# Linear-attention and SwiGLU kernel: zeros on TensorE ahead of the first tile, a written order for four token tiles, phi's small add on GpSimd

## Chip, cores and metric

One Trainium2 chip, one of its cores. The metric is the time of one execution in microseconds (us), as the device reports it; lower is better. Of the profiled execution, the span runs from the first to the last instruction of the program.

## What is computed

A block of x (2048 tokens by 1024, bf16) is layer-normalised, put through linear attention with 32 heads of 32 columns, and gated by a SwiGLU network whose output goes through one more silu:

```python
xn = layernorm(x)                      # eps 1e-5
q, k, v = split(xn @ wqkv)             # 32 heads of 32
phi = lambda t: where(t > 0, t + 1, exp(t)) + 1e-6
kv = einsum("bhsd,bhse->bhde", phi(k), v)
z = einsum("bhsd->bhd", phi(k))
o = einsum("bhqd,bhde->bhqe", phi(q), kv) / (phi(q) . z + 1e-6)
s = o @ wo
g = silu((silu(xn @ w_gate) * (xn @ w_up)) @ w_down)    # F = 3584
out = x + s * g
```

The sums kv and z run over all 2048 tokens, so no query can be finished before the last token's K and V are known.

## The kernel before

**Stages.** Tokens go in 16 tiles of 128 (four to a block). Stage 1, the K/V stage: each tile is normalised to `xn` (fp16), transposed on TensorE (`emit_A2`, L289; eight 128x128 transposes into one PSUM bank, copied to `xnT` by VectorE, L300), then multiplied with four chunks of 512 columns of the K/V weights `wkv_sb` (`emit_B`, L315; eight matmuls a chunk, L322): chunks 0 and 1 are K, 2 and 3 are V. A K chunk goes through phi (`emit_phi`, L121): ScalarE takes exp (L123) and relu (L125) of the PSUM bank into `e_t` and `r_t`, VectorE adds 1e-6 to `r_t` (L126) and forms min(e_t, 1) + r_t (L127). A V chunk is copied by ScalarE (L330). `emit_C` (L333) multiplies phi(k) with V into `kvz_ps`, eight small products a tile. From token 1024 on, `xn` is transposed by a DMA over `xn_dram` (L310, L311) instead of TensorE. Stage 2: 32 products for q (`emit_Q`, L142, phi again), products with kv and z (`emit_ND`, L416) and, after a DMA transpose of o, the product with wo (`emit_S`, L449), whose result goes to `s_dram`. The first eight Q tiles run before the first `emit_ND`; VectorE forms the first sums of FFN weights (`sum_w`, L629 to L633) beside them. Stage 3 is the FFN as seven products of halves (L511), two thirds of the time.

**Normalisation.** `emit_stats` (L233) makes two `bn_stats` and one `bn_aggr` a tile. Tiles 0 and 1 take the root on ScalarE (`emit_rstd_act`, L255). Tiles 2 and 3 one by one, and later tiles four together, take it by three Newton rounds on VectorE (`emit_rstd`, L262), operations on 128x1 or 128x4. `emit_norm` (L283) applies it.

**Buffers.** PSUM: `psB` has three banks for K/V chunks, q and s products; `psC` two for transposes; `psA` three for kvz. `e_t`, `r_t`, `xn` and `pk_sb` have two buffers each, V two (`v_bufs`).

**What sets the order.** Each engine runs its own list in order. In stages 1 and 2 a planner with its own costs writes the lists from the program's order and the dependencies; the loop at L362 gives that order: tile i's chunk 0, `emit_C` of tile i - 1, the other chunks, then tile i + 2's normalisation and transposes. In VectorE's list that comes out as the first half of tile 2's `bn_stats` ahead of tile 1's `bn_aggr`. In stage 3 the order of TensorE and GpSimd is written out by hand.

**Loads.** SyncE (SP) issues x tile 0 (its second half is issued by ScalarE, L188), K/V chunk 0 in two halves, then x1, chunk 1, x2, chunk 2, x3, chunk 3, x4 and the other x tiles (L200 to L209). `wq_sb` and `wo_sb` (L210, L212) and the stores to `s_dram` (L462) are issued from GpSimd's queue (POOL). Gates hold x8 on until tile 1's first chunk, wq until tile 3's, wo until tile 5's.

Of the kernel before, what the change touches and what calls it, by code (L numbers as in the profile page):

```python
# [9 lines left out]
ACT = mybir.ActivationFunctionType  # L10
ALU = mybir.AluOpType
# [10 lines left out]
def kernel(  # L22
# [64 lines left out]

    nc.scalar.preload_act_table(ACT.Sqrt)
    ident = persist.tile([P, P], FP16, name="ident")
    make_identity(nc, ident[:])  # L90
# [29 lines left out]

    def emit_phi(work, t_ps, dst, W):  # L121
        e_t = work.tile([P, W], FP32, name="e_t", tag="e_t")
        ex = nc.scalar.activation(out=e_t[:], in_=t_ps, func=ACT.Exp)  # L123
        r_t = work.tile([P, W], FP32, name="r_t", tag="r_t")
        nc.scalar.activation(out=r_t[:], in_=t_ps, func=ACT.Relu)  # L125
        nc.vector.tensor_scalar(out=r_t[:], in0=r_t[:], scalar1=EPS, scalar2=None, op0=ALU.add)  # L126
        nc.vector.scalar_tensor_tensor(out=dst, in0=e_t[:], scalar=1.0, in1=r_t[:],  # L127
                                       op0=ALU.min, op1=ALU.add)
        return ex
# [35 lines left out]
    with ExitStack() as p1:  # L165
# [4 lines left out]
        wkv_sb = wpool.tile([P, DC, 2 * D], BF16, name="wkv_sb")  # L170
        v_bufs = [wpool.tile([P, G, NDW], BF16, name=f"v_sb{k}") for k in range(2)]
        for k in range(2):
            nc.gpsimd.memset(v_bufs[k][:, :, P:P + 1], 1.0)
# [27 lines left out]
        load_wkv(0, halves=2 if DC % 2 == 0 else 1)  # L201
        nx = 1
        for c in range(1, NCH):
# [4 lines left out]
        for i in range(nx, NT):  # L208
            load_x(i)  # L209
        wq_loads = [nc.gpsimd.dma_start(out=wq_sb[:, :, c * CW:(c + 1) * CW], in_=wqkv_v[:, :, c * CW:(c + 1) * CW])  # L210
                    for c in range(NCC)]
        wo_loads = [nc.gpsimd.dma_start(out=wo_sb[:, :, c * CW:(c + 1) * CW], in_=wo_v[:, :, c * CW:(c + 1) * CW])  # L212
                    for c in range(NCC)]
# [19 lines left out]
        def emit_stats(i):  # L233
# [9 lines left out]
            sts = [nc.vector.bn_stats(out=stats[:, c, :], in_=xr[:, c, :]) for c in range(NSC)]  # L243
            if TPB <= i < 2 * TPB:
                late_gates.append((sts, ("B", min(1, NT - 1))))
            nc.vector.bn_aggr(out=mv[:, k, :], in_=stats[:])
# [15 lines left out]
        def emit_rstd(gid):  # L262
            mv, rstd, tiles = grp_state[gid]
            n = len(tiles)
            a = small.tile([P, TPB], FP32, name="lna", tag="lna")
            nc.vector.tensor_scalar(out=a[:, 0:n], in0=mv[:, 0:n, 1], scalar1=EPS_LN, scalar2=None, op0=ALU.add)
            yi = rstd[:, 0:n].bitcast(I32)
            nc.vector.tensor_single_scalar(out=yi, in_=a[:, 0:n].bitcast(I32), scalar=1, op=ALU.arith_shift_right)
            nc.vector.tensor_scalar(out=yi, in0=yi, scalar1=-1, scalar2=0x5f3759df, op0=ALU.mult, op1=ALU.add)
            y = rstd[:, 0:n]  # L270
            w = small.tile([P, TPB], FP32, name="lnw", tag="lnw")
            for _ in range(NR_ITERS):
                if n == 1:
                    nc.vector.scalar_tensor_tensor(out=w[:, 0:1], in0=y, scalar=a[:, 0:1], in1=y,
                                                   op0=ALU.mult, op1=ALU.mult)
                else:
                    nc.vector.tensor_tensor(out=w[:, 0:n], in0=y, in1=y, op=ALU.mult)
                    nc.vector.tensor_tensor(out=w[:, 0:n], in0=w[:, 0:n], in1=a[:, 0:n], op=ALU.mult)
                nc.vector.tensor_scalar(out=w[:, 0:n], in0=w[:, 0:n], scalar1=-0.5, scalar2=1.5,
                                        op0=ALU.mult, op1=ALU.add)  # L280
                nc.vector.tensor_tensor(out=y, in0=y, in1=w[:, 0:n], op=ALU.mult)

# [5 lines left out]

        def emit_A2(i):  # L289
            xn = work.tile([P, D], FP16, name="xn", tag="xn")  # L290
            tr_ps = psC.tile([P, DC, P], FP16, name="tr_ps", tag="C")
            nh = 2 if (i == 0 and DC % 2 == 0) else 1
            dch = DC // nh
            cp = None
            for hh in range(nh):
                cols = slice(hh * dch * P, (hh + 1) * dch * P)
                emit_norm(i, xn[:, cols], cols=(cols if nh > 1 else None))
                for dc in range(hh * dch, (hh + 1) * dch):
                    nc.tensor.transpose(tr_ps[:, dc, :], xn[:, dc * P:(dc + 1) * P], ident[:])  # L299
                cp = nc.vector.tensor_copy(out=xn_tok_ap(i)[:, hh * dch:(hh + 1) * dch, :],  # L300
                                           in_=tr_ps[:, hh * dch:(hh + 1) * dch, :])
            ln_state.pop(i)
            return cp

        def emit_A2_block(b):
# [8 lines left out]

        def emit_B(i, c):  # L315
            if i not in pkv_tiles:
                pk_sb = work.tile([P, D], BF16, name="pk_sb", tag="pk_sb")
                pkv_tiles[i] = (pk_sb, v_bufs[i % 2])
            pk_sb, v_sb = pkv_tiles[i]
            kv_ps = psB.tile([P, CW], FP32, name="kv_ps", tag="B")  # L320
            for dc in range(DC):
                mm = nc.tensor.matmul(kv_ps[:], lhsT=xn_tok_ap(i)[:, dc, :], rhs=wkv_sb[:, dc, c * CW:(c + 1) * CW],  # L322
                                      start=(dc == 0), stop=(dc == DC - 1))
                if dc == 0 and c == 0:
                    marks[("B", i)] = mm
            if c < NCC:
                return emit_phi(phiw, kv_ps[:], pk_sb[:, c * CW:(c + 1) * CW], CW)
            else:
                vc = c - NCC
                return nc.scalar.copy(out=v_sb[:, vc * GPC:(vc + 1) * GPC, 0:P],  # L330
                                      in_=kv_ps[:].rearrange("p (g c) -> p g c", c=P))

# [17 lines left out]
        NPE = min(PE_T_BLOCKS * TPB, NT)  # L350
        cp0 = None
        sq_last = None
        for i in range(min(2, NT)):
            sts = emit_stats(i)
            nstat = i + 1
            if i > 0:
                gate(sts, cp0)
            sq_last = emit_rstd_act(grp_of(i))
            cp = emit_A2(i)
            if i == 0:  # L360
                cp0 = cp
        for i in range(NT):  # L362
            ex = emit_B(i, 0)
            if i == 0:
                gate([ex], sq_last)
            if i > 0:
# [6 lines left out]
            if nxt < NPE:  # L373
                if nxt < TPB:
                    stats_upto(nxt + 1)
                    emit_rstd(grp_of(nxt))
                elif nxt % TPB == 0:
                    stats_upto(nxt + TPB)
                    emit_rstd(grp_of(nxt))
                emit_A2(nxt)  # L380
# [26 lines left out]
    with ExitStack() as p2:  # L407
# [41 lines left out]
        def emit_S(b, t, cc):  # L449
# [10 lines left out]
            if cc == NCC - 1:  # L460
                r0 = b * TB + t * P
                nc.gpsimd.dma_start(out=s_dram[r0:r0 + P, :], in_=s_tiles.pop((b, t))[:])  # L462

# [386 lines left out]
```

## Time and profile before

| what | value |
|---|---|
| time, median of 3 (lowest to highest) | 770.65 us (770.33 to 770.73) |
| profiled execution: time, span | 770.58 us, 768.7 us |
| TensorE (PE) busy | 750.0 us (98%) |
| VectorE (DVE) busy | 485.4 us (63%) |
| ScalarE (ACT) busy | 266.9 us (35%) |
| GpSimd (POOL) busy | 51.8 us (7%) |
| mean granted TensorE clock | 0.996 |

The 1.9 us between time and span lie outside the program's instructions. In the rows of the timeline come: start from the span's start (us), length (us), engine, line, operation, what is written <- what is read, the count of instructions merged into the row, and in brackets the engine's idle time before it with what ended it. A PE row's busy time is modelled, so the spacing of starts tells the pace. PEld is TensorE's weight load; SPq, POOLq are queues that issue DMAs.

### The profile page before, as it was taken

How to read it: one execution, taken by the hardware profiler on the slowest of the kernel's cores; microseconds unless marked ns; L12 is line 12 of the kernel's file. 1: busy time of each engine (PE TensorE's matmuls, PEld its weight loads, DVE VectorE, ACT ScalarE, POOL GpSimd, SP SyncE). 2: the span in 40 equal slices, each digit the busy share in tenths (PEclk: the TensorE clock that was granted, in tenths of full speed). 3: DMA queues.
4: the chain of work that ended last, by engine and by line, in shares of the span. 5: the costliest groups of instructions: out<-in, count | busy, mean ns of one | idle time of the engine just before them, and what ended most of it. 6: DMA issues, size and time to landing. Idle time of an engine off the chain costs nothing.

```text
span 768.7 us, 9747 instructions
## 1 busy us (share of the span) xinstructions
PE 750.0 (98%) x3661; PEld 349.8 (46%) x3696; DVE 485.4 (63%) x987; ACT 266.9 (35%) x461; POOL 51.8 (7%) x61
## 2 busy tenths in 40 slices
PE   5999999999999999999999999999999999999996
PEld 2444444455544444444444444444444444444442
DVE  6994223899760387677876778767655654445542
ACT  2444444555333433433334333343434011111111
POOL 0010000000011000000000000000000221222222
PEclk9999999999999999999999999999999999999999
DMA  9349044014661155553555535453969955544200
GB/s 317 121 155 267 18 108 111 1 41 136 170 203 71 51 160 158 157 170 94 168 150 156 166 104 172 143 153 100 321 185 317 361 179 179 178 177 171 90 28 28
DMA packets 122560, 115.99 MB, mean 151 GB/s; under 512 B 28560, under 2 KB 103184, under 8 KB 121232
## 3 DMA queue, kind: packets, MB, share of 16 engines
q1 hardware_dynamic: 120000, 106.84, 44.8%
q0 software_dynamic: 2368, 8.39, 3.2%
q8 instruction: 29, 0.48, 0.3%
q14 instruction: 19, 0.16, 0.1%
q10 hardware_dynamic: 144, 0.13, 0.0%
HBM read 70.52 MB, written 38.54 MB: 142 GB/s over the span
## 4 chain that ended last, share of the span: by engine, by line
PE 94%; DVE 3%; DMA 1%; issue 1%; SPq 0%; ACT 0%; POOLq 0%; POOL 0%; DVEq 0%
PE X L511 28%; PE Y L511 28%; PE kv_ps L322 12%; PE Z L511 9%; PE q_ps L148 7%; PE s_ps L457 7%; DVE stats L243 2%; DMA xp<-in_A_x_dram 1%; PE nd_ps L429 1%; PE kvz L337 1%; PE tr_ps L299 0%; DVE pk_sb L127 0%; DVE r_t L126 0%; SPq L194 0%; DVE xn L286 0%
## 5 line engine op out<-in xcount | busy, mean ns | idle before, releaser
L511 PEld LDWEIGHTS <-ws_all 128*128 128x128 bf16 x1232 | 120.6, 98 | 145.3
L531 DVE TENSOR_TENSOR q<-n,Y 128x512 f32<-128x512 f32 x64 | 44.0, 687 | 139.9 <-PE Y L511 109.7
L322 PE MATMUL kv_ps<-wkv_sb,xnT 128*128 128x512 bf16 x499 | 116.6, 386 | 1.1 <-DMA wkv_sb<-in_A_wqkv_dram 0.5
L511 PEld LDWEIGHTS <-xs 128*128 128x128 bf16 x560 | 54.8, 98 | 66.1
L322 PEld LDWEIGHTS <-xnT 128*128 128x128 f16 x512 | 49.9, 99 | 57.6 <-issue 4.5
L793 POOL TENSOR_TENSOR o_out<-y,xres 128x512 bf16<-128x512 f32 x32 | 38.6, 1206 | 471.0 <-DVE y L792 471.0
L511 PE MATMUL X<-xnT,ws_all 128*128 128x512 f16 (+1 forms) x278 | 70.1, 379 | 0.2
L511 PE MATMUL Y<-xs,ws_all 128*128 128x512 f16 (+1 forms) x280 | 70.2, 379 | 0.0
L126 DVE TENSOR_SCALAR r_t<-r_t 128x512 f32<-128x512 f32 x64 | 26.9, 420 | 49.4 <-ACT r_t L125 49.4
L511 PE MATMUL Z<-xs,ws_all 128*128 128x512 f16 x224 | 57.5, 379 | 0.0
L511 PE MATMUL Y<-xnT,ws_all 128*128 128x512 f16 x224 | 57.5, 379 | 0.0
L511 PE MATMUL X<-xs,ws_all 128*128 128x512 f16 x224 | 57.5, 379 | 0.0
L148 PE MATMUL q_ps<-xnT,wq_sb 128*128 128x512 f16 x256 | 57.3, 379 | 0.0
L457 PE MATMUL s_ps<-wo_sb,oT 128*128 128x512 bf16 x250 | 55.7, 379 | 0.3
L537 DVE TENSOR_TENSOR u<-Z,q 128x512 f32<-128x512 f32 x64 | 43.8, 685 | 18.3 <-PE Z L511 18.1
L649 ACT ACTIVATE g<-cg 128x512 bf16<-128x512 f32 x56 | 35.3, 631 | 54.4 <-DVE cg L546 54.4
L649 ACT ACTIVATE g<-X 128x512 bf16<-128x512 f32 x28 | 16.7, 597 | 99.9 <-PE X L511 99.9
L527 ACT COPY n<-X 128x512 f32<-128x512 f32 x64 | 37.5, 586 | 29.0 <-PE X L511 29.0
L674 DVE TENSOR_TENSOR ho<-g,up 128x1024 bf16<-128x1024 bf16 x56 | 38.1, 683 | 0.5
L457 PEld LDWEIGHTS <-oT 128*128 128x128 bf16 x256 | 24.9, 98 | 29.0
L792 DVE TENSOR_TENSOR y<-y,s_in 128x512 f32<-128x512 f32 x32 | 22.9, 715 | 23.0 <-ACT y L791 18.9
L148 PEld LDWEIGHTS <-wq_sb 128*128 128x128 bf16 x256 | 24.5, 98 | 27.2
(107 smaller groups left out, 948.1 us busy)
## 6 DMA issues: line engine op xcount, KB each, us to landing
h_dram<-ho SPq DMA_DIRECT2D x56, 256.0 KB, 2.6
wg_sb<-in_B_w_gate_dram SPq DMA_DIRECT2D x14, 512.0 KB, 4.0
wu_sb<-in_B_w_up_dram SPq DMA_DIRECT2D x14, 512.0 KB, 4.8
wdr<-in_B_w_down_dram SPq DMA_DIRECT2D x14, 512.0 KB, 4.1
ws_all<-h_dram SPq DMA_DIRECT2D x4, 1792.0 KB, 8.9
wds_dram<-wdsA SPq DMA_DIRECT2D x14, 384.0 KB, 2.9
hp_a<-h_dram SPq DMA_DIRECT2D x3, 1792.0 KB, 8.6
o_dram<-o_blk SPq DMA_DIRECT2D x4, 1024.0 KB, 4.4
```

Source lines behind the costliest of these rows:

```text
L126: nc.vector.tensor_scalar(out=r_t[:], in0=r_t[:], scalar1=EPS, scalar2=None, op0=ALU.add)
L148: nc.tensor.matmul(q_ps[:], lhsT=wq_sb[:, dc, g * P:(g + 1) * P], rhs=xn_blk_ap(b)[:, dc, :], start=(dc == 0), stop=(dc == DC - 1))
L322: mm = nc.tensor.matmul(kv_ps[:], lhsT=xn_tok_ap(i)[:, dc, :], rhs=wkv_sb[:, dc, c * CW:(c + 1) * CW], start=(dc == 0), stop=(dc == DC - 1))
L457: nc.tensor.matmul(s_ps[:], lhsT=oT[:, c, ttok], rhs=wo_sb[:, c, cc * CW:(cc + 1) * CW], start=(c == 0), stop=(c == G - 1))
L511: marks["mm"] = nc.tensor.matmul(acc[:], lhsT=lhs(k), rhs=rhs(k), start=(first and k == 0), stop=(k == n - 1), skip_group_check=True)
L527: nc.scalar.copy(out=n[:], in_=self.X[:])
L531: nc.vector.tensor_tensor(out=self.q[:], in0=n[:], in1=self.Y[:], op=ALU.add)
L537: nc.vector.tensor_tensor(out=self.u[:], in0=Z[:], in1=self.q[:], op=ALU.add)
L649: nc.scalar.activation(out=self.g[:, i, j * TB:(j + 1) * TB], in_=src, func=ACT.Silu)
L674: nc.vector.tensor_tensor(out=self.ho[:, i], in0=self.g[:, i], in1=self.up[:, i], op=ALU.mult)
L792: nc.vector.tensor_tensor(out=t[:], in0=t[:], in1=self.s_in[:, i, cs], op=ALU.mult)
L793: nc.gpsimd.tensor_tensor(out=self.o_out[:, i, cs], in0=t[:], in1=self.xres[:, i, cs], op=ALU.add)
```

## The change

1. **Zeros.** VectorE clears a tile `warm`, and TensorE multiplies it with itself: 14 matmuls ahead of tile 0's transposes, 2 after them, 5 after chunk 0 of tile 0. Their bank `w_ps` is one of psB's three and is never read.
2. **A written order** for PE, DVE, ACT and POOL over tiles 0 to 3: after chunk 0 of tile 0 the tiles share each chunk of weights: (0,1) (1,0) (1,1) (0,2) (1,2) (2,0) (2,1) (2,2) (0,3) (1,3) (2,3), as (tile, chunk), with tile 2's and 3's transposes between. Then the planner goes on with tile 3 and, inside it, the transposes of tiles 4 and 5. For that, `emit_B` is split into its matmuls and its way out, `emit_A2` into normalisation and transposes; V and `pk_sb` get four buffers.
3. **Normalisation.** Tile 0's transposes use two banks. Each tile's transposed block is copied half by VectorE, half by ScalarE. The Newton rounds of tiles 2 and 3 move to GpSimd, with the fused operation split in two: 24 operations. ScalarE's table for exp is loaded after tile 1's root. The statistics of later blocks have other due points.
4. **Loads and stores.** x2 is issued ahead of K/V chunk 1. wq, wo and the stores to `s_dram` go from POOL's queue to SP's.
5. **phi.** The add of 1e-6 runs on GpSimd in 58 of 64 cases; six K chunks of tiles 0 to 2 keep it on VectorE.

```diff
     nc.scalar.preload_act_table(ACT.Sqrt)
+    warm = persist.tile([P, TB], BF16, name="warm")
+    nc.vector.memset(warm[:], 0.0)
...
-    def emit_phi(work, t_ps, dst, W):
+    def emit_phi(work, t_ps, dst, W, eng=None):
         e_t = work.tile([P, W], FP32, name="e_t", tag="e_t")
         ex = nc.scalar.activation(out=e_t[:], in_=t_ps, func=ACT.Exp)
         r_t = work.tile([P, W], FP32, name="r_t", tag="r_t")
         nc.scalar.activation(out=r_t[:], in_=t_ps, func=ACT.Relu)
-        nc.vector.tensor_scalar(out=r_t[:], in0=r_t[:], scalar1=EPS, scalar2=None, op0=ALU.add)
+        (eng or nc.gpsimd).tensor_scalar(out=r_t[:], in0=r_t[:], scalar1=EPS, scalar2=None, op0=ALU.add)
         nc.vector.scalar_tensor_tensor(out=dst, in0=e_t[:], scalar=1.0, in1=r_t[:],
                                        op0=ALU.min, op1=ALU.add)
...
-        v_bufs = [wpool.tile([P, G, NDW], BF16, name=f"v_sb{k}") for k in range(2)]
-        for k in range(2):
+        v_bufs = [wpool.tile([P, G, NDW], BF16, name=f"v_sb{k}") for k in range(4)]
+        for k in range(4):
...
         load_x(0)
         load_wkv(0, halves=2 if DC % 2 == 0 else 1)
-        nx = 1
+        load_x(1)
+        nx = 2
         for c in range(1, NCH):
             if nx < NT:
                 load_x(nx)
@@ -207,9 +210,9 @@
             load_wkv(c)
         for i in range(nx, NT):
             load_x(i)
-        wq_loads = [nc.gpsimd.dma_start(out=wq_sb[:, :, c * CW:(c + 1) * CW], in_=wqkv_v[:, :, c * CW:(c + 1) * CW])
+        wq_loads = [nc.sync.dma_start(out=wq_sb[:, :, c * CW:(c + 1) * CW], in_=wqkv_v[:, :, c * CW:(c + 1) * CW])
                     for c in range(NCC)]
-        wo_loads = [nc.gpsimd.dma_start(out=wo_sb[:, :, c * CW:(c + 1) * CW], in_=wo_v[:, :, c * CW:(c + 1) * CW])
+        wo_loads = [nc.sync.dma_start(out=wo_sb[:, :, c * CW:(c + 1) * CW], in_=wo_v[:, :, c * CW:(c + 1) * CW])
                     for c in range(NCC)]
...
-            if TPB <= i < 2 * TPB:
-                late_gates.append((sts, ("B", min(1, NT - 1))))
+            if i >= TPB:
+                late_gates.append((sts, "T3" if i < 2 * TPB else ("B", i // TPB * 3 - 3)))
...
+            eng = nc.gpsimd if n == 1 else nc.vector
...
-                if n == 1:
-                    nc.vector.scalar_tensor_tensor(out=w[:, 0:1], in0=y, scalar=a[:, 0:1], in1=y,
-                                                   op0=ALU.mult, op1=ALU.mult)
-                else:
-                    nc.vector.tensor_tensor(out=w[:, 0:n], in0=y, in1=y, op=ALU.mult)
-                    nc.vector.tensor_tensor(out=w[:, 0:n], in0=w[:, 0:n], in1=a[:, 0:n], op=ALU.mult)
-                nc.vector.tensor_scalar(out=w[:, 0:n], in0=w[:, 0:n], scalar1=-0.5, scalar2=1.5,
+                eng.tensor_tensor(out=w[:, 0:n], in0=y, in1=y, op=ALU.mult)
+                eng.tensor_tensor(out=w[:, 0:n], in0=w[:, 0:n], in1=a[:, 0:n], op=ALU.mult)
+                eng.tensor_scalar(out=w[:, 0:n], in0=w[:, 0:n], scalar1=-0.5, scalar2=1.5,
                                         op0=ALU.mult, op1=ALU.add)
-                nc.vector.tensor_tensor(out=y, in0=y, in1=w[:, 0:n], op=ALU.mult)
+                eng.tensor_tensor(out=y, in0=y, in1=w[:, 0:n], op=ALU.mult)
...
-        def emit_A2(i):
-            xn = work.tile([P, D], FP16, name="xn", tag="xn")
-            tr_ps = psC.tile([P, DC, P], FP16, name="tr_ps", tag="C")
-            nh = 2 if (i == 0 and DC % 2 == 0) else 1
-            dch = DC // nh
-            cp = None
-            for hh in range(nh):
-                cols = slice(hh * dch * P, (hh + 1) * dch * P)
-                emit_norm(i, xn[:, cols], cols=(cols if nh > 1 else None))
-                for dc in range(hh * dch, (hh + 1) * dch):
-                    nc.tensor.transpose(tr_ps[:, dc, :], xn[:, dc * P:(dc + 1) * P], ident[:])
-                cp = nc.vector.tensor_copy(out=xn_tok_ap(i)[:, hh * dch:(hh + 1) * dch, :],
-                                           in_=tr_ps[:, hh * dch:(hh + 1) * dch, :])
+        xn_tiles = {}
+
+        def emit_N(i):
+            xn_tiles[i] = work.tile([P, D], FP16, name="xn", tag="xn")
+            emit_norm(i, xn_tiles[i][:])
+
+        def emit_T(i):
+
+            h = DC // 2
+            dst = xn_tok_ap(i)
+
+            def tr(t_ps, dcs):
+                for k, dc in enumerate(dcs):
+                    nc.tensor.transpose(t_ps[:, k, :], xn[:, dc * P:(dc + 1) * P], ident[:])
+
+            if i == 0:
+                xn = work.tile([P, D], FP16, name="xn", tag="xn")
+                tr_a = psC.tile([P, h, P], FP16, name="tr_ps", tag="C")[:]
+                tr_b = psC.tile([P, h, P], FP16, name="tr_ps", tag="C")[:]
+                emit_norm(i, xn[:, 0:h * P], cols=slice(0, h * P))
+                tr(tr_a, range(0, h))
+                emit_norm(i, xn[:, h * P:D], cols=slice(h * P, D))
+                tr(tr_b, range(h, DC))
+            else:
+                xn = xn_tiles.pop(i)
+                tr_ps = psC.tile([P, DC, P], FP16, name="tr_ps", tag="C")
+                tr_a, tr_b = tr_ps[:, 0:h, :], tr_ps[:, h:DC, :]
+                tr(tr_ps, range(DC))
+            cp = nc.vector.tensor_copy(out=dst[:, 0:h, :], in_=tr_a)
+            nc.scalar.copy(out=dst[:, h:DC, :], in_=tr_b)
             ln_state.pop(i)
             return cp
+
+        def emit_A2(i):
+            emit_N(i)
+            emit_T(i)
...
-        def emit_B(i, c):
+        kv_tiles = {}
+
+        def emit_B_mm(i, c):
             if i not in pkv_tiles:
-                pk_sb = work.tile([P, D], BF16, name="pk_sb", tag="pk_sb")
-                pkv_tiles[i] = (pk_sb, v_bufs[i % 2])
-            pk_sb, v_sb = pkv_tiles[i]
+                pk_sb = work.tile([P, D], BF16, name="pk_sb", tag="pk_sb", bufs=4)
+                pkv_tiles[i] = (pk_sb, v_bufs[i % 4])
             kv_ps = psB.tile([P, CW], FP32, name="kv_ps", tag="B")
             for dc in range(DC):
                 mm = nc.tensor.matmul(kv_ps[:], lhsT=xn_tok_ap(i)[:, dc, :], rhs=wkv_sb[:, dc, c * CW:(c + 1) * CW],
                                       start=(dc == 0), stop=(dc == DC - 1))
                 if dc == 0 and c == 0:
                     marks[("B", i)] = mm
+            kv_tiles[(i, c)] = kv_ps
+
+        def emit_B_out(i, c, eng=None):
+            pk_sb, v_sb = pkv_tiles[i]
+            kv_ps = kv_tiles.pop((i, c))
             if c < NCC:
-                return emit_phi(phiw, kv_ps[:], pk_sb[:, c * CW:(c + 1) * CW], CW)
+                emit_phi(phiw, kv_ps[:], pk_sb[:, c * CW:(c + 1) * CW], CW, eng)
             else:
                 vc = c - NCC
-                return nc.scalar.copy(out=v_sb[:, vc * GPC:(vc + 1) * GPC, 0:P],
-                                      in_=kv_ps[:].rearrange("p (g c) -> p g c", c=P))
+                nc.scalar.copy(out=v_sb[:, vc * GPC:(vc + 1) * GPC, 0:P],
+                               in_=kv_ps[:].rearrange("p (g c) -> p g c", c=P))
+
+        def emit_B(i, c):
+            emit_B_mm(i, c)
+            emit_B_out(i, c)
...
-        cp0 = None
-        sq_last = None
-        for i in range(min(2, NT)):
-            sts = emit_stats(i)
-            nstat = i + 1
-            if i > 0:
-                gate(sts, cp0)
-            sq_last = emit_rstd_act(grp_of(i))
-            cp = emit_A2(i)
-            if i == 0:
-                cp0 = cp
-        for i in range(NT):
-            ex = emit_B(i, 0)
-            if i == 0:
-                gate([ex], sq_last)
+        w_ps = psB.tile([P, TB], FP32, name="w_ps", tag="B")
+
+        def warm_up(n):
+            for _ in range(n):
+                nc.tensor.matmul(w_ps[:], lhsT=warm[:, 0:P], rhs=warm[:], start=True, stop=True)
+
+        def ln(i):
+            emit_stats(i)
+            (emit_rstd_act if i < 2 else emit_rstd)(i)
+
+
+        ET = mybir.EngineType
+        with tc.manual_schedule(engines={ET.PE, ET.DVE, ET.Activation, ET.Pool}):
+            warm_up(14)
+            ln(0)
+            emit_T(0)
+            warm_up(2)
+            emit_B_mm(0, 0)
+            warm_up(5)
+            ln(1)
+            nc.scalar.preload_act_table(ACT.Exp)
+            emit_N(1)
+            emit_T(1)
+            emit_B_mm(0, 1)
+            ln(2)
+            emit_B_mm(1, 0)
+            ln(3)
+            emit_B_out(0, 0, nc.vector)
+            emit_B_mm(1, 1)
+            emit_N(2)
+            emit_B_out(0, 1, nc.vector)
+            emit_B_out(1, 0, nc.vector)
+            emit_B_mm(0, 2)
+            emit_T(2)
+            emit_B_out(1, 1, nc.vector)
+            emit_B_out(0, 2, nc.vector)
+            emit_B_mm(1, 2)
+            emit_N(3)
+            emit_B_mm(2, 0)
+            emit_B_out(1, 2, nc.vector)
+            marks["T3"] = emit_T(3)
+            emit_B_mm(2, 1)
+            emit_B_out(2, 0, nc.vector)
+            emit_B_mm(2, 2)
+            emit_B_out(2, 1, nc.vector)
+            emit_B_mm(0, 3)
+            emit_B_out(2, 2, nc.vector)
+            emit_B_mm(1, 3)
+            emit_B_out(0, 3, nc.vector)
+            emit_C(0)
+            nstat = TPB
+            emit_B_mm(2, 3)
+            emit_B_out(1, 3, nc.vector)
+            emit_C(1)
+        stats_upto(2 * TPB)
+        emit_rstd(grp_of(TPB))
+        emit_B_out(2, 3)
+        for c in range(NCH):
+            emit_B(3, c)
+            if c == 0:
+                emit_C(2)
+            if c in (1, 2):
+                emit_A2(TPB + c - 1)
+        for i in range(TPB, NT):
+            emit_B(i, 0)
             if i > 0:
                 emit_C(i - 1)
             for c in range(1, NCH):
@@ -371,12 +452,6 @@
                 emit_B(i, c)
             nxt = i + 2
             if nxt < NPE:
-                if nxt < TPB:
-                    stats_upto(nxt + 1)
-                    emit_rstd(grp_of(nxt))
-                elif nxt % TPB == 0:
-                    stats_upto(nxt + TPB)
-                    emit_rstd(grp_of(nxt))
                 emit_A2(nxt)
...
-                nc.gpsimd.dma_start(out=s_dram[r0:r0 + P, :], in_=s_tiles.pop((b, t))[:])
+                nc.sync.dma_start(out=s_dram[r0:r0 + P, :], in_=s_tiles.pop((b, t))[:])
```

`late_gates` names the point at which a planner may place later tiles' statistics; `marks["T3"]` is VectorE's copy of tile 3's transposed block.

## The prediction, on record before the result

> **What bounds it now.** I read the page first: the forty slices, then the chain of waits.
>
> ```profile
> PE   5999999999999999999999999999999999999996
> DVE  6994223899760387677876778767655654445542
> POOL 0010000000011000000000000000000221222222
> ...
> PE 94%; DVE 3%; DMA 1%; issue 1%; SPq 0%; ACT 0%; POOLq 0%; POOL 0%; DVEq 0%
> ```
>
> TensorE (PE) is full in every slice of 19 us but the first and the last, and the chain is 94% PE. An edit outside the first slices can win nothing; it can only lose, by making PE wait. So I went to the timeline (start us, length us, engine, line, operation, tiles, count, idle before it and what ended that) for every wait of PE:
>
> ```profile
> 3.50 1.29 DVE L243 BATCH_NORM_STATS2 stats<-xp 128x6 f32<-128x512 bf16 x2 [1.59 <-DMA xp<-in_A_x_dram]
> ...
> 6.13 0.61 PE L299 MATMUL tr_ps<-ident,xn 128*128 128x128 f16 x4 [6.13 <-DVE xn L286]
> ...
> 7.63 3.53 PE L322 MATMUL kv_ps<-wkv_sb,xnT 128*128 128x512 bf16 x8
> ...
> 8.65 1.28 DVE L243 BATCH_NORM_STATS2 stats<-xp 128x6 f32<-128x512 bf16 x2 [0.35 <-DMA xp<-in_A_x_dram]
> ...
> 11.67 1.24 PE L322 MATMUL kv_ps<-wkv_sb,xnT 128*128 128x512 bf16 x5 [0.50 <-DMA wkv_sb<-in_A_wqkv_dram]
> ...
> 12.34 0.70 DVE L243 BATCH_NORM_STATS2 stats<-xp 128x6 f32<-128x512 bf16 x1 [2.40 <-DMA xp<-in_A_x_dram]
> ...
> 14.42 1.03 PE L299 MATMUL tr_ps<-ident,xn 128*128 128x128 f16 x8 [1.51 <-DVE lna L266]
> ```
>
> The reader is to see that PE starts at 6.13, and that at 12.34 VectorE (DVE) stands 2.40 us on x tile 2 with tile 1's mean still unfinished behind it, so tile 1's transposes come at 14.42. Later there is one more wait, for tile 4:
>
> ```profile
> 43.32 0.62 PE L299 MATMUL tr_ps<-ident,xn 128*128 128x128 f16 x8 [1.10 <-DVE xn L286]
> ```
>
> The first matmuls are spaced 3.53/8 = 0.44 us; later ones take 6.91 us for 32, that is 0.216. The clock row says why, by stretches of 3.41 us (columns: PE, PEld, DVE, ACT, POOL busy, then the clock):
>
> ```profile
> 10.95:14.36 3.41, 1.46 (x6) 0.38 (x4) 2.02 (x7) 1.16 (x2) 0.00 (x0) 1.00 1.08 356
> 14.37:17.77 3.40, 3.35 (x14) 1.74 (x15) 3.01 (x11) 2.49 (x5) 0.00 (x0) 0.50 1.08 357
> ```
>
> After a stretch with PE busy for 43%, the granted clock was 0.50 for one stretch.
>
> I count PE's **lost time**: the moment less the work done, priced at full speed: a chunk (8 matmuls, L322) 1.73 us, eight transposes 0.45, eight products into kvz 0.46 (spacings at 38.79 and 43.32). When tile 4's transposes start at 43.32, PE has issued 117 matmuls of chunks (25.27), 32 transposes (1.80) and 24 kvz products (1.38): 28.45 of work, **14.9 us lost**. After 43.32 PE waits nowhere over 0.06 us.
>
> **The new start, step by step.** I work through the four lists as written, with durations of before.
>
> Loads: x2 is moved ahead of K/V chunk 1. Chunk 0 and x1 are unmoved, so x1 lands at 8.63 (the wait at 8.65). Chunk 1 lands when before's x2 did, with the same bytes ahead: 12.3 (before 11.6). From there 0.7 us per x tile and 3.0 per chunk, by the same waits: x3 13.0, chunk 2 16.0, chunk 3 19.7.
>
> Zeros: 14 matmuls from 1.2, at 0.43 done by 7.2, earlier if the clock rises. Tile 0's transposes, ready at 6.13, may wait 1.1 us; this costs nothing, since after chunk (0,0) (done 9.2 to 10.4) and five more zeros PE must wait anyway. Tile 1: stats 8.65 to 9.94, then 0.87 to the normalisation (4.79 to 5.66 on tile 0), 0.50 for it: transposes 11.4, copies 12.6 (ScalarE's after its table load, 1.28). Chunk (0,1) starts with its weights at 12.3. Lost so far: 12.3 less 1.73 and 0.9, **9.7 us**. Then (1,0) 14.1, (1,1) 15.8, (0,2) 17.5 to 19.3, each with weights there and its bank cleared.
>
> VectorE: after tile 1's copy (12.45) stats of tile 2 and three small ones (0.18 apart) to 14.65, of tile 3 to 16.7, phi(0,0) to 17.8, then the normalisation of tile 2, which waits for GpSimd (POOL): 12 dependent operations on 128x1 (four, three rounds). No row shows these. The ends: 0.10, a 128x1 memset on POOL (L253), and 1.15, a 128x512 TENSOR_TENSOR there (L793). The nearest is one input of 128 elements:
>
> ```profile
> masks.py:199 POOL TENSOR_SCALAR_AFFINE_SELECT ident<-ident 128x128 f16<-128x128 f16 x1 | 0.3, 288 | 0.0
> ...
> L253 POOL MEMSET eps_ln<- 128x1 f32 x1 | 0.1, 102 | 0.0
> ```
>
> I take 0.25 with the hand-over: tile 2 done at 17.7, tile 3 at 20.7. Behind the waiting normalisation stand (0,1)'s and (1,0)'s phi, and behind those the buffers that ScalarE's next exponential needs. At 0.25 nothing waits: tile 2 normalised 18.4, transposes at 19.3 on time, (1,2) to 21.5, (2,0) from 21.8 (ScalarE clears (1,1)'s bank at 21.7), tile 3's transposes at 23.5. Work by then: 7 chunks 12.1, 24 transposes 1.35; lost **10.05**. I add 0.3 for POOL and VectorE blocking each other (below): 10.35. Tile 4: VectorE has 8 stats (5.1), four aggregates, two phi, 15 small operations and one normalisation, done near 35; its transposes come at 37.4, so the old 1.1 us wait is gone with 2.4 in hand. **Start: 14.9 - 10.35 = 4.5 us gained.**
>
> The other loads: wq, wo and s_dram go from POOL's queue to SP's. wq's gate comes near 34, wanted at 137; the transposing load of tokens 1024 on now queues behind wo, whose gate (tile 5) comes near 50 and whose 2 MB take 6 us at chunk 0's pace: it would start near 56, takes 7.7 to 15.6 from issue to landing (the two L311 loads; the long one beside wo) and is wanted near 72. s_dram writes (16) queue behind the o_dram pairs, and only h-stage loads that wait for slots stand behind. I cost all at 0; without that cover a late transpose is a direct PE wait.
>
> **The 58 adds on POOL.** In the K/V and mixed stages there is room. The first eight Q tiles are the tight place:
>
> ```profile
> 137.00:150.00 13.00, 13.00 (x64) 5.90 (x61) 12.96 (x32) 7.60 (x14) 0.00 (x0) 1.00 0.01 1
> ```
>
> DVE is full there, with 16 sums of weights (L629 to L633, 6.5 us) between the phi. Taking L126 (0.33 spacing) away gives room, but two engines that read SBUF get in each other's way:
>
> ```profile
> 609.15 2.81 POOL L793 TENSOR_TENSOR o_out<-y,xres 128x512 bf16<-128x512 f32 x1 [353.04 <-DVE y L792]
> ...
> 610.86 1.64 DVE L792 TENSOR_TENSOR y<-y,s_in 128x512 f32<-128x512 f32 x1
> ```
>
> L793 takes 1.15 alone and L792 0.68. Here L793 came while L761 (two SBUF inputs, 608.93 to 610.95) ran and took 2.81; L792 came while L793 ran and took 1.64: each waits out the other. L127 and the sums also have two SBUF inputs. So per Q tile, for about 4.5 tiles, sums 1.3, L127 0.6 and the add stand one after another against 1.73 of PE; three PSUM banks cover 3.46. The add on POOL is in no row: 0.42 (L126 on DVE) to 1.15 (L793, two inputs). Cost 4.5 x (1.9 + add - 1.73) - 3.46, not below 0: nothing at 0.42, 2.5 us at 1.15. I take 0.75, towards the middle, as it reads half of what L793 reads: **0.7 us lost**. With ND between the Q tiles two tiles have 3.92 us, enough up to 1.15.
> The Trainium skill (GPSIMD Engine Reference, section 4.1) calls one-input operations there roughly line rate, at 1.2 GHz an estimate of 0.43 us; by that the stage costs 0 and the sum is 766.1. No run here shows it.
>
> **Sum.** 770.58 (span 768.7 and 1.9 around it) - 4.5 + 0.7 = **766.8 us**. That execution lies 0.07 under the median 770.65, so the same serves for the median.
>
> **Rivals.** (1) The clock falls back. PE idles about 1.2 us before tile 1's transposes and 0.5 before chunk (0,1); in an unlucky stretch that leaves 50% busy, near the 43% that dropped it before. Price: one stretch at half speed, 1.7 us: 768.5. For it, the row above; against, the zeros fill part.
> The Trainium skill (TensorE: Matmul & The Clock Gate, Part 1) has the clock fall after an idle window of about 3.4 us; by that this rival is void and 766.8 stands. The trace disagrees: the stretch before its drop was 43% busy.
> (2) Slower: POOL's 24 small operations. Tile 3's transposes come no earlier than 15.25 + 24p. Up to p = 0.34 nothing is late; at 0.55 the gain is gone; at 0.8 they come at 34.5, 10.7 late: 777.4; at 1.15, 785. For it: L793, and that each waits for the one before; against: the memsets.
> (3) Nothing: the gain is made and given back, with p at 0.4 (1.4 late) and the add at 1.15 (1.8 more): 770.0.
>
> **Chances.** Forecast 0.60 (764.8 with an add of 0.42 and chunk 1 a us earlier, to 768.3 with the add at 1.1); rival 1 0.16; rival 2 0.13; rival 3 0.11. The range 764.8 to 769.8 takes in the first two and part of the third. A measurement tells about 0.2% (1.5 us) from no change: faster 0.78, same 0.09, slower 0.13.
>
> **What would show it.** Right: chunk (0,1) starts at 12.3 on a weight load; tile 3's transposes near 23.5; no wait at tile 4; PE waits under 1 us between 132 and 146; POOL adds 0.6 to 0.9. Wrong: PE waiting for xn of tile 2 or 3 with POOL's small operations over 0.35; a second stretch of clock 0.50; adds over 1.1 and PE gaps among the Q tiles.

## The result and the profile after

The changed kernel takes 773.85 us (median of 4 runs, 772.66 to 774.11) beside 770.49 us before (4 runs, 769.52 to 770.73). The ratio is 1.0046, with a 95% interval of 1.0033 to 1.0058: **slower by about 3.4 us**, where 766.8 was forecast. The profiled execution took 774.11 us, with a span of 772.3 (before: 770.58 and 768.7). The page of the kernel after, forty slices and chain:

```profile
PE   8999999899999999999999999999999999999996
...
DVE  5877212678780287686876868767755654454542
...
POOL 2143433789500000000000000000000221212222
...
PE 87%; DVE 5%; POOL 3%; issue 2%; DMA 1%; ACT 1%; SPq 0%; POOLq 0%; DVEq 0%; ACTq 0%
```

Two things are new. PE's first slice is filled (8 instead of 5), as meant. But PE dips in the eighth slice (135 to 154 us), where it was full before; POOL goes from 3 to 7 there and to 9 two slices on, and the chain now has 3% of POOL in it. The start in the timeline of PE:

```profile
1.17 4.87 PE L386 MATMUL w_ps<-warm 128*128 128x512 bf16 x14 [1.17 <-DVE warm L90]
...
8.81 1.02 PE L344 MATMUL kv_ps<-wkv_sb,xnT 128*128 128x512 bf16 x4 [0.54 <-DMA wkv_sb<-in_A_wqkv_dram]
...
12.17 0.62 PE L302 MATMUL tr_ps<-ident,xn 128*128 128x128 f16 x8 [1.25 <-DVE xn L286]
13.18 7.07 PE L344 MATMUL kv_ps<-wkv_sb,xnT 128*128 128x512 bf16 x31 [0.39 <-DMA wkv_sb<-in_A_wqkv_dram]
...
23.88 1.89 PE L344 MATMUL kv_ps<-wkv_sb,xnT 128*128 128x512 bf16 x7 [1.46 <-ACT r_t L127]
25.61 0.61 PE L302 MATMUL tr_ps<-ident,xn 128*128 128x128 f16 x8
```

Chunk (0,1) starts at 13.18, when the DMA of its weights lands, as forecast, but 0.9 later; chunk (2,0) waits 1.46 us, where 0.3 had been allowed; tile 3's transposes come at 25.61, not 23.5. The wait for tile 4 is gone. Less 13.45 us of work, PE has lost 12.16 us by then, and 14.9 before: the start wins **2.7 us**. What led to the 1.46 stands in the lists of VectorE and ScalarE:

```profile
19.22 0.55 DVE L286 TENSOR_SCALAR xn<-xp,mv,rstd 128x1024 f16<-128x1024 bf16 x1 [0.91 <-POOL rstd L281]
...
22.26 0.58 ACT L318 COPY xnT<-tr_ps 128x512 f16<-128x512 f16 x1 [2.74 <-DVE xnT L317]
```

VectorE stands 0.91 on POOL's small operations before it can normalise tile 2, and works without a break from there to its half of tile 2's copy. ScalarE stands before its own half of that copy until then, with the exponential of (1,1) behind it, and chunk (2,0) needs (1,1)'s bank.

Now the rows around the first ND, the first products of q with kv and z (all engines):

```profile
147.91 9.78 POOL L128 TENSOR_SCALAR r_t<-r_t 128x512 f32<-128x512 f32 x5 [0.93 <-ACT r_t L127]
...
149.43 0.69 DVE L129 SCALAR_TENSOR_TENSOR pqT<-e_t,r_t 128x512 bf16<-128x512 f32 x1 [1.51 <-POOL r_t L128]
...
151.51 0.69 DVE L129 SCALAR_TENSOR_TENSOR pqT<-e_t,r_t 128x512 bf16<-128x512 f32 x1 [1.38 <-POOL r_t L128]
...
153.58 0.69 DVE L129 SCALAR_TENSOR_TENSOR pqT<-e_t,r_t 128x512 bf16<-128x512 f32 x1 [1.38 <-POOL r_t L128]
...
154.33 0.23 PE L504 MATMUL nd_ps<-KVZ,pqT 128*128 128x132 bf16 x1 [1.84 <-DVE pqT L129]
```

VectorE is idle 1.38 us before each phi, and what it waits for is POOL's add; POOL works without a break, five adds in 9.78 us. Phi comes every 2.07 us, where PE makes a Q tile every 1.73. The first ND reads all eight tiles of the block, and its last matmul waits 1.84 us for the eighth. The clock follows (stretches; PE, PEld, DVE, ACT, POOL busy, then clock):

```profile
151.36:154.77 3.41, 1.16 (x11) 0.67 (x10) 1.39 (x2) 1.49 (x3) 3.25 (x3) 1.00 0.00 0
154.78:158.18 3.40, 3.40 (x9) 1.21 (x8) 2.53 (x8) 1.18 (x4) 2.83 (x2) 0.50 0.00 0
```

PE was busy for 34% of one stretch, and in the next one the clock was at 0.50, which costs 1.7 us.

To place the loss I compared the start of each of PE's weight loads (PEld) with the same one before: 2.71 us early from tile 8 to the eighth Q tile; 1.83 late after the first ND; 2.63 late after the 72nd ND matmul, 3.53 after the 104th, and constant from there to the end. So the stage gives back 4.54 at the first ND (eight ND matmuls in 3.07 us instead of 0.47, the clock 1.7, a rest of 0.2) and 0.8 and 0.9 later, at two more waits for `pqT`: 770.58 - 2.71 + 6.25 = 774.1. The groups of POOL give the price:

```profile
L868 POOL TENSOR_TENSOR o_out<-y,xres 128x512 bf16<-128x512 f32 x32 | 38.6, 1206 | 526.7 <-DVE y L867 526.7
...
L128 POOL TENSOR_SCALAR r_t<-r_t 128x512 f32<-128x512 f32 x58 | 99.6, 1717 | 80.8 <-ACT r_t L127 70.5
```

The add has a mean of 1.72 us: **1.49 alone**, 1.99 where VectorE's L129 starts with it. With one input it is dearer than L868 with two.

### The profile page after: what moved, and what is told of

Its sections match the earlier page's. It is cut to its first block, busy times and chain, and to the rows that moved or that the text cites. A ratio compares the mean times of both kernels' runs of the same rounds, so it can differ in the third digit from the quotient of the medians.

```text
span 772.3 us, 9832 instructions
## 1 busy us (share of the span) xinstructions
PE 755.2 (98%) x3681; PEld 351.3 (45%) x3717; DVE 470.5 (61%) x911; ACT 270.7 (35%) x469; POOL 145.5 (19%) x125
## 4 chain that ended last, share of the span: by engine, by line
PE 87%; DVE 5%; POOL 3%; issue 2%; DMA 1%; ACT 1%; SPq 0%; POOLq 0%; DVEq 0%; ACTq 0%
PE X L586 28%; PE Y L586 28%; PE kv_ps L344 12%; PE Z L586 9%; PE s_ps L532 7%; POOL r_t L128 3%; DVE pqT L129 1%; PE q_ps L150 1%; DVE o_blk L512 1%; DMA xp<-in_A_x_dram 1%; PE kvz L368 1%; PE tr_ps L302 0%; PE nd_ps L504 0%; DVE stats L246 0%; DVE rden L511 0%
## 5 line engine op out<-in xcount | busy, mean ns | idle before, releaser
L868 POOL TENSOR_TENSOR o_out<-y,xres 128x512 bf16<-128x512 f32 x32 | 38.6, 1206 | 526.7 <-DVE y L867 526.7
L344 PE MATMUL kv_ps<-wkv_sb,xnT 128*128 128x512 bf16 x498 | 113.7, 379 | 3.1 <-ACT r_t L127 1.5
L128 POOL TENSOR_SCALAR r_t<-r_t 128x512 f32<-128x512 f32 x58 | 99.6, 1717 | 80.8 <-ACT r_t L127 70.5
L150 PE MATMUL q_ps<-xnT,wq_sb 128*128 128x512 f16 x256 | 59.2, 387 | 0.1
L129 DVE SCALAR_TENSOR_TENSOR pk_sb<-e_t,r_t 128x512 bf16<-128x512 f32 x32 | 21.9, 687 | 53.7 <-POOL r_t L128 53.6
```

Of the source, the lines that this page charges most:

```text
L128: (eng or nc.gpsimd).tensor_scalar(out=r_t[:], in0=r_t[:], scalar1=EPS, scalar2=None, op0=ALU.add)
L150: nc.tensor.matmul(q_ps[:], lhsT=wq_sb[:, dc, g * P:(g + 1) * P], rhs=xn_blk_ap(b)[:, dc, :], start=(dc == 0), stop=(dc == DC - 1))
L868: nc.gpsimd.tensor_tensor(out=self.o_out[:, i, cs], in0=t[:], in1=self.xres[:, i, cs], op=ALU.add)
```

## The experiments

The theory after this reading: the 58 adds lose the time, by their rate in Q; all else gains. Each ratio below is against the kernel before, run beside it on the same chip. "Given back" is read from the weight-load starts as above.

**1. The Q adds alone back on VectorE** (e1_q_add_dve).

```diff
-        emit_phi(phiw, q_ps[:], pqT[:, g, :], TB)
+        emit_phi(phiw, q_ps[:], pqT[:, g, :], TB, nc.vector)
```

> The changed kernel, with the add of 1e-6 for the 32 Q tiles back on VectorE; everything else is as changed. Theory A (the loss is GpSimd's add in the Q stage: 1.49 us alone, 2.07 a tile when VectorE's phi runs beside it, against 1.73 to 1.96 of TensorE): the start's gain of 2.7 us stays and nothing is given back, no PE wait from 133 on, time 770.5 - 2.7 = 767.8, ratio 0.9965. Rival B (the loss comes from moving wq, wo and the s_dram stores to SP, or from the planner's other order after tile 3, and the adds only stand beside it): the time stays within 1 us of 773.9.

Measured: 766.84 us, ratio 0.9947 (0.9932 to 0.9963). PE's timeline:

```profile
133.79 15.70 PE L150 MATMUL q_ps<-xnT,wq_sb 128*128 128x512 f16 x72
149.33 0.63 PE L504 MATMUL nd_ps<-KVZ,pqT 128*128 128x132 bf16 x8
```

The eight ND matmuls follow without a wait. PE is 4.45 us early at tile 8 and stays so to the end: nothing is given back. All 26 other adds are still on POOL, and nothing of PE's lead is lost to them. That the loss lies in the 32 Q adds is shown.

**2. The kernel before, with its 64 adds on POOL and no other edit** (e2_before_pool_add).

```diff
-        nc.vector.tensor_scalar(out=r_t[:], in0=r_t[:], scalar1=EPS, scalar2=None, op0=ALU.add)
+        nc.gpsimd.tensor_scalar(out=r_t[:], in0=r_t[:], scalar1=EPS, scalar2=None, op0=ALU.add)
```

> The kernel before, with one edit: all 64 adds of 1e-6 on GpSimd. Theory A: the Q stage loses what it loses in the changed kernel, about 6.2 us, and the first tiles up to 1 us more, since phi is on the way to their PSUM banks: 776.7 to 777.7, ratio 1.008 to 1.009. Rival B: below 772, since the loads and the order are those of before.

Measured: 779.61 us, ratio 1.0115 (1.0097 to 1.0132), some 2 us above what was expected. PE's timeline:

```profile
45.00 0.62 PE L299 MATMUL tr_ps<-ident,xn 128*128 128x128 f16 x8 [2.97 <-DVE xn L286]
157.52 0.23 PE L429 MATMUL nd_ps<-KVZ,pqT 128*128 128x132 bf16 x1 [0.41 <-DVE pqT L127]
159.59 0.23 PE L429 MATMUL nd_ps<-KVZ,pqT 128*128 128x132 bf16 x1 [1.84 <-DVE pqT L127]
```

The waits at the first ND, 0.41 and 1.84, are those of the changed kernel to the hundredth, with 4.54 given back there and 6.33 in all. The other 2.55 are lost in the start: 1.9 where tile 4 now waits 2.97 instead of 1.10; the other 0.7 is about what chunk 1 landed later in this execution (12.37, before 11.62). The 1.9 is not shown to be the price of the adds themselves: VectorE stands on POOL only 0.64 and 0.72 us (for phi of tile 0), and the planner wrote VectorE's list anew for this edit, with 30 `bn_stats` ahead of tile 4's normalisation instead of 28.

**3. Three buffers for e_t and r_t.** The rival: phi waits for buffers, not for POOL's rate (e3_phi_three).

```diff
-    phiw = p12.enter_context(tc.tile_pool(name="phiw", bufs=2))
+    phiw = p12.enter_context(tc.tile_pool(name="phiw", bufs=3))
```

> The changed kernel with three buffers each for e_t and r_t in place of two. Rival C (the Q stage is held by the length of the loop exp, relu, add, phi over two buffers, not by GpSimd's rate): a third buffer takes the loop off, the Q stage loses under 1 us: 768 to 769. Theory A with the rate as the bound (an add of 1.49 stretched to 1.99 by the phi beside it, 2.07 from add to add, over 1.96 of TensorE): a third buffer only puts the wait off; the Q stage still loses 3 to 6 us: 771 to 774.

Measured: 773.94 us, ratio 1.0041 (1.0026 to 1.0056). POOL's timeline, then PE's:

```profile
137.72 18.41 POOL L128 TENSOR_SCALAR r_t<-r_t 128x512 f32<-128x512 f32 x9 [0.24 <-ACT r_t L127]
```

```profile
152.77 0.23 PE L504 MATMUL nd_ps<-KVZ,pqT 128*128 128x132 bf16 x1 [1.84 <-DVE pqT L129]
```

Nine adds run back to back at 2.05 us each, and the wait is still 1.84. The buffers are not the bound; the rate is. The time is the changed kernel's partly by chance: this execution's start won 3.6 us, the Q blocks gave back 5.6 (3.9 of it at the first ND), and another 1.4 went at the start of the FFN, where PE waits 1.19 for a sum of weights on VectorE, which it does not in the changed kernel.

**4. Whole copies.** In the start, ScalarE's half of tile 2's copy, which queues behind VectorE's, led to the wait of 1.46. Here VectorE copies the whole block from tile 1 on, on top of experiment 1 (e4_copy_dve).

```diff
+            if i == 0:
                 cp = nc.vector.tensor_copy(out=dst[:, 0:h, :], in_=tr_a)
                 nc.scalar.copy(out=dst[:, h:DC, :], in_=tr_b)
+            else:
+                cp = nc.vector.tensor_copy(out=dst, in_=tr_ps[:])
```

> As e1_q_add_dve, and from tile 1 on VectorE copies the whole transposed block (0.68 us) and ScalarE none of it. Theory D (the 1.46 us that TensorE waits before chunk (2,0) come from ScalarE standing on its half of tile 2's copy, which waits for VectorE's half behind two phi, with exp of (1,1) queued behind it): the wait shrinks to 0.2 or less and the time is 1.2 us under e1, 766.6. Rival: the wait is VectorE's own lateness, and the longer copy makes it 0.3 worse: e1 plus 0.3.

Measured: 765.96 us, ratio 0.9938 (0.992 to 0.9956); its interval overlaps that of experiment 1. The trace:

```profile
21.53 1.90 PE L347 MATMUL kv_ps<-wkv_sb,xnT 128*128 128x512 bf16 x7 [0.38 <-ACT v_sb L360]
...
23.17 0.55 DVE L286 TENSOR_SCALAR xn<-xp,mv,rstd 128x1024 f16<-128x1024 bf16 x1 [0.64 <-POOL rstd L281]
...
23.77 0.62 PE L302 MATMUL tr_ps<-ident,xn 128*128 128x128 f16 x8 [0.35 <-DVE xn L286]
```

The wait of 1.46 falls to 0.38, but 0.35 appears ahead of tile 3's transposes, because tile 3's normalisation now stands 0.64 on POOL's small operations. From chunk (0,1) to these takes 11.9 us instead of 12.4: 0.5 won in the trace, under half of what was expected, and not shown by the times.

**5. Exponentials in PSUM.** Is the add slow beside phi because both read SBUF (e5_exp_psum)? In block 0, phi's exponential goes to PSUM, and L129 (L132 here) then has one input in SBUF.

```diff
-        e_t = work.tile([P, W], FP32, name="e_t", tag="e_t")
+        if e_pool is None:
+            e_t = work.tile([P, W], FP32, name="e_t", tag="e_t")
+        else:
+            e_t = e_pool.tile([P, W], FP32, name="e_ps", tag="C")
...
-        emit_phi(phiw, q_ps[:], pqT[:, g, :], TB)
+        emit_phi(phiw, q_ps[:], pqT[:, g, :], TB, e_pool=psC if b == 0 else None)
```

> The changed kernel, with one difference: for the eight Q tiles of block 0, ScalarE writes its exponential to a PSUM tile instead of SBUF, so that VectorE's closing step of phi reads only one operand from SBUF. The 58 adds stay on GpSimd. Theory (two engines that read SBUF in VectorE's two-operand form and GpSimd's form block each other): the adds of these eight tiles go from 1.99 us to about 1.5, add to add falls from 2.07 to under 1.75, the first ND finds its data in time or nearly so, and the wait of 1.84 and the clock's fall behind it go; the later waits (0.8 and 0.9) stay: 769.0 to 770.5 us. Rival (the add is that slow of itself, whatever runs beside it): 773 to 774.5 us, adds at 1.9 to 2.0 as before.

Measured: 770.02 us, ratio 0.9999 (0.9989 to 1.0009). POOL's timeline, then VectorE's and PE's:

```profile
143.66 1.49 POOL L131 TENSOR_SCALAR r_t<-r_t 128x512 f32<-128x512 f32 x1 [0.38 <-DVE ws_all L708]
145.53 3.09 POOL L131 TENSOR_SCALAR r_t<-r_t 128x512 f32<-128x512 f32 x2 [0.38 <-ACT r_t L130]
149.00 3.05 POOL L131 TENSOR_SCALAR r_t<-r_t 128x512 f32<-128x512 f32 x2 [0.38 <-ACT r_t L130]
```

and VectorE's phi, which starts 0.08 before the second add of the second row:

```profile
147.05 0.69 DVE L132 SCALAR_TENSOR_TENSOR pqT<-e_ps,r_t 128x512 bf16<-128x512 f32 x1 [1.18 <-POOL r_t L131]
```

PE's:

```profile
151.27 0.23 PE L507 MATMUL nd_ps<-KVZ,pqT 128*128 128x132 bf16 x1 [0.34 <-DVE pqT L132]
...
183.94 0.23 PE L507 MATMUL nd_ps<-KVZ,pqT 128*128 128x132 bf16 x1 [0.73 <-DVE pqT L132]
200.52 0.23 PE L507 MATMUL nd_ps<-KVZ,pqT 128*128 128x132 bf16 x1 [0.73 <-DVE pqT L132]
```

The adds beside phi take 1.49 now, two of them 3.47 us from start to start, which is PE's pace; POOL has time to spare. The wait at the first ND is 0.34, the clock stays at 1.00, and 0.5 is given back there instead of 4.54. The later blocks still read two inputs from SBUF, and their waits stay. So 0.5 us of each add that starts with phi is the two engines blocking each other, shown. The Trainium skill (SBUF — State Buffer, "Who interferes with whom") says so: a VectorE instruction with two SBUF inputs contends with a GpSimd instruction that reads SBUF; one with at most one, outside the two-port modes, does not. These traces agree, 1.99 against 1.49, for operations that start together. Being beside each other for a while is not enough: two sums of weights, with both inputs in SBUF, start 0.53 and 0.86 us into the add of 143.66, and it took 1.49 and they 0.41 each, as alone.

**6. Two inputs for the add** (e6_add_two_inputs).

```diff
-        (eng or nc.gpsimd).tensor_scalar(out=r_t[:], in0=r_t[:], scalar1=EPS, scalar2=None, op0=ALU.add)
+        if eng is None:
+            nc.gpsimd.tensor_tensor(out=r_t[:], in0=r_t[:], in1=eps_row[:], op=ALU.add)
+        else:
+            eng.tensor_scalar(out=r_t[:], in0=r_t[:], scalar1=EPS, scalar2=None, op0=ALU.add)
```

> The changed kernel, with GpSimd's add as an operation of two inputs, r_t plus a row that holds 1e-6, in place of an operation of one input and a constant. In the kernel before, a two-input 128x512 operation on GpSimd took 1.15 us alone; the one-input add of the changed kernel takes 1.49 alone and 1.99 beside VectorE. Theory (the price of the add decides the Q stage): at 1.15 alone and about 1.65 beside phi, eight tiles take no longer than TensorE's 1.73 each, the first ND is not late and the clock does not fall: 768 to 769.5 us. Rival (the kind of operation does not matter, 128x512 floats on GpSimd are slow as such, the 1.15 was of another mix of types): 773 to 774.5 us.

Measured: 767.52 us, ratio 0.997 (0.9959 to 0.9981), the changed kernel's 58 adds all still on POOL. The group of the adds, then PE's timeline:

```profile
L129 POOL TENSOR_TENSOR r_t<-r_t,eps_row 128x512 f32<-128x512 f32 x58 | 82.8, 1427 | 91.3 <-ACT r_t L127 89.9 <-DVE o_blk L518 0.3
```

```profile
151.26 0.23 PE L510 MATMUL nd_ps<-KVZ,pqT 128*128 128x132 bf16 x1 [0.27 <-DVE pqT L132]
```

The same sum with one more input is faster: 1.26 to 1.27 alone (1.15 had been expected), 1.73 beside phi in block 0, 1.86 from add to add. The one wait left in the Q blocks is 0.27.

| kernel | add alone, beside phi | mean from phi to phi, block 0 | given back at first ND, in all Q blocks |
|---|---|---|---|
| changed | 1.49, 1.99 | 2.13 | 4.54, 6.25 |
| exponentials in PSUM | 1.49, 1.49 | 1.79 | 0.51, 2.73 |
| add with two inputs | 1.26, 1.73 | 1.85 | 0.45, 0.45 |
| Q adds on VectorE | none on POOL | 1.70 | 0, 0 |

The loss follows the spacing of the eight phi, seven steps: 0.40 above PE's 1.73 is 2.8 us, with the clock's 1.7 behind it 4.5; 0.06 and 0.12 above it cost 0.5 and leave the clock at 1.00.

**7 to 9. Parts of the start,** each on top of experiment 4. No zeros (e7_no_zeros):

```diff
-            for _ in range(n):
+            for _ in range(0):
```

> The changed kernel with the Q adds on VectorE and whole copies on VectorE (it took 765.96 us), and without the 21 matmuls on zeros at the start. Theory 1 (the zeros earn their place): TensorE starts at a clock of 0.5, the first 3.4 to 7 us of its work take twice as long, of which some lies before the wait for chunk 1 anyway: chunk (0,0) then ends about 1.8 us later, but chunk (0,1) waits for its weights; the clock may fall once more in the stretch after: 766.5 to 768.5 us. Theory 2 (hidden by the load of chunk 1): 765.5 to 766.3 us, no difference.

Measured: 766.26 us, ratio 0.9957 (0.9945 to 0.997): no difference that can be measured from experiment 4. PE's timeline without zeros:

```profile
6.05 1.03 PE L302 MATMUL tr_ps<-ident,xn 128*128 128x128 f16 x8 [6.05 <-DVE xn L286]
7.17 3.51 PE L347 MATMUL kv_ps<-wkv_sb,xnT 128*128 128x512 bf16 x8
10.80 0.62 PE L302 MATMUL tr_ps<-ident,xn 128*128 128x128 f16 x8
```

Chunk (0,0) takes twice as long, but is done by 10.7, and tile 1's transposes start at 10.80 instead of 10.87: the zeros only fill a wait.

Newton rounds of tiles 2 and 3 on VectorE (e8_newton_dve):

```diff
-            eng = nc.gpsimd if n == 1 else nc.vector
+            eng = nc.vector
```

> The same kernel of 765.96 us, with the Newton rounds of tiles 2 and 3 (24 operations on 128x1) on VectorE instead of GpSimd. Theory 1 (VectorE is the fuller list in the start): 24 operations at about 0.18 us are 4.4 us more on VectorE; with the waits for GpSimd gone (0.9 us and more) tile 2's transposes come 1 to 2 us later and chunk (2,0) with them: 767 to 768.5 us. Theory 2 (the hand-over to GpSimd costs as much as the work): 765.3 to 766.3 us.

Measured: 770.85 us, ratio 1.0013 (1.0004 to 1.0021); the gain is gone, far more than the 1 to 2 us I expected.

```profile
23.17 0.62 PE L302 MATMUL tr_ps<-ident,xn 128*128 128x128 f16 x8 [3.48 <-DVE xn L286]
```

Both tiles' rounds stand ahead of tile 2's normalisation in VectorE's written list, 24 operations at 0.19 or 4.6 us, and little of that finds cover: tile 2's transposes wait 3.48, and come 10.6 us after chunk (0,1) instead of 6.9; tile 3's come 15.0 after it instead of 11.9. In this execution 0.7 us was left of the start's 4.5; another 0.7 is chunk 1, which landed later than in experiment 4. With this written order, moving the rounds to POOL is what carries the start; another order with the rounds on VectorE was not run.

The loads in the old order, chunk 1 ahead of x2 (e9_loads_back):

```diff
         load_x(0)
         load_wkv(0, halves=2 if DC % 2 == 0 else 1)
-        load_x(1)
-        nx = 2
+        nx = 1
```

> The kernel of 765.96 us (changed kernel, Q adds and whole copies on VectorE), with the loads back in the order of the kernel before: x tile 2 behind K/V chunk 1 instead of ahead of it. Theory 1 (the landing of chunk 1 sets the start): chunk 1 lands 0.7 us earlier, near 11.2, so chunk (0,1) starts when tile 1 is transposed, near 11.4 instead of 11.88, and 0.4 to 0.5 us is won: 765.4 to 765.6 us, with x tile 2 at about 11.9 still ahead of its place in VectorE's list at 12.3. Theory 2 (what VectorE has to do before tiles 2 and 3 sets the start): tile 3's transposes stay at 23.8, the waits ahead of chunk (2,0) and of these transposes grow by what (0,1) won: 765.8 to 766.2 us, no gain.

Measured: 767.05 us (765.5 to 767.35), ratio 0.9943 (0.9929 to 0.9957), the same as experiment 4.

```profile
10.64 7.07 PE L346 MATMUL kv_ps<-wkv_sb,xnT 128*128 128x512 bf16 x31
...
14.87 1.29 DVE L245 BATCH_NORM_STATS2 stats<-xp 128x6 f32<-128x512 bf16 x2 [1.34 <-DMA xp<-in_A_x_dram]
...
18.54 0.62 PE L301 MATMUL tr_ps<-ident,xn 128*128 128x128 f16 x8 [0.83 <-DVE xn L285]
```

Chunk (0,1) starts at 10.64, 1.24 earlier than in experiment 4, half of it because all loads came earlier in this execution; tile 2's transposes then wait 0.83 for VectorE, and tile 3's come only 0.53 earlier. The second theory was right that there is no gain, but not on the reason: VectorE stood 1.34 us on the load of x tile 3, which now comes behind chunk 2 and landed at 14.85 (12.53 in experiment 4), and tile 3's statistics stand ahead of tile 2's normalisation in its list. What the old order wins on chunk 1 it loses on x3.

## Why the prediction was wrong, point by point

- **PE is full, so only the start can win:** right, and so was the warning beside it that other edits can only lose. The start gave no more than 4.5 us in the changed kernel or experiment 1.
- **Start, 4.5 us forecast, 2.7 measured.** Of the missing 1.8, 0.9 is the load: chunk 1 landed at 13.14, not 12.3. That moves from one execution to the next: in the six kernels with this load order in experiments 1 and 3 to 7, chunk 1 landed between 11.39 and 12.43, and the start won 3.4 to 4.6 us. In experiment 1's execution (11.39) it was 4.45, the forecast nearly to the tenth, but by luck: chunk 1 came 0.9 earlier than I had put it, and that paid for the 1.46, which was there as well. The other 0.9 is the wait of 1.46 ahead of chunk (2,0), less the 0.3 I had allowed and some slack. Two steps lie behind it: I gave ScalarE's half of tile 2's copy no place in its queue, and POOL's small operations were dearer than I took them (next point). Experiment 4 removed the first and won 0.5.
- **POOL's small operations at 0.25:** too cheap, though a small part of the miss. Undisturbed they come 0.27 to 0.28 apart, but beside VectorE some take 0.4 to 0.65, and the 24 took 8.25 us, 0.34 each (0.37 in experiment 4). Up to 0.34 nothing was to be late; tile 2's normalisation waited 0.91 for them, and in experiment 4 tile 3's 0.64 and PE 0.35 behind it, which I had named as a sign of being wrong. Rival 2 needed 0.55 throughout to lose the gain, and that did not happen; experiment 8 shows the move to be worth over 3 us.
- **Other loads at 0:** right; with the Q adds away, PE's lead stays at 4.45 from tile 8 to the end.
- **The 58 adds, 0.7 us forecast, 6.25 measured. This step failed, at the price of the add.** I took 0.75, between 0.42 and a two-input operation's 1.15, since one input should cost less than two. It costs 1.49, outside the range. My formula at 1.49 would have said 4.0 and the sum 770.1, close to the 4.54 of the first ND. It did so partly by luck: it had the sums of weights as the third party and POOL waiting its turn behind them, but the sums end by 147.3 and the chain of add and phi, 2.07 a tile, is late on its own (in experiment 3 its phi come 2.07 apart from the first on, sums or not). It had no clock in it (1.7 of the 4.54). "Enough up to 1.15" for the later blocks stands (at 1.26, in experiment 6, nothing is late there), but two chains of 2.07 are 4.14 against 3.92, hence the later 0.8 and 0.9.
- The Trainium skill (GPSIMD Engine Reference, section 4.1) calls one-input operations roughly line rate, an estimate of 0.43 us here. The trace disagrees: 1.49 alone.
- **Rival 1, the clock:** right in kind, wrong in place. It did not fall in the start; it fell after the first ND's wait. The Trainium skill (TensorE: Matmul & The Clock Gate, Part 1) speaks of an idle window of about 3.4 us. The trace disagrees: the stretch of 3.41 us before the fall was 34% busy, with no idle time over 1.84.
- **Rival 3, nothing:** nearest in mechanism, a gain made and given back, but its add of 1.15 was too cheap to end on the other side. My slower case was tied to the wrong operations on POOL: the 24 small ones, and not the 58 large ones.

What stays open: why the one-input add is slower than the two-input one on POOL, what sets the moment at which the first loads land, and how little of a stretch TensorE must be busy for the clock to fall.

## What to carry to other kernels

An operation of another engine that no row shows has no upper bound in a "larger" operation of that engine; its price decides, so measure that one form first. Where two engines work in turn on a tile and both read SBUF, add their times (here 1.49 and 0.69, 2.18 where 2.07 was measured), and compare the sum with TensorE's pace per tile. A stage that is full on TensorE and has a burst without a break (here eight Q tiles ahead of the first ND) is where such a chain comes late, and the wait can cost a stretch of clock on top.

## What the runs showed of the hardware

- On GpSimd, 128x512 float32 plus a constant took 1.49 us, plus a second tensor 1.26 to 1.27; with a bfloat16 result (L868) 1.15.
- Such an add took 0.5 us longer when VectorE's phi with two SBUF inputs started with it, and no longer when one of those inputs was in PSUM.
- On GpSimd, dependent operations on 128x1 float32 came 0.27 to 0.28 us apart, and took up to 0.65 beside VectorE; on VectorE they came 0.19 apart (experiment 8).
- The clock fell to 0.50 for one stretch of 3.4 us after a stretch with TensorE 34% busy, in mid kernel, with no single idle time over 1.84 us.
- The second half of the first weight chunk landed between 6.79 and 8.77 us among the profiled executions, and chunk 1 in the new load order 4.36 to 4.37 after it each time.
